# Attention state advanced on TensorE by diagonal products, and a list of work with its weight conversions moved

## The chip, the cores and the metric

One core of a Trainium2 chip. The metric is device time in microseconds (us) from launch to end, the median of several runs of the same kernel. A core has TensorE (PE in the rows; its weight loads are PEld), VectorE (DVE), ScalarE (ACT), GpSimd (POOL) and SyncE (SP), each with its own instruction queue, in order; a name with a q (SPq, ACTq) is the part of an engine that issues DMAs and waits. TensorE writes to PSUM, in banks of 128 partitions x 512 fp32.

## The reference

Three stages in a row, in fp32, checked against a numpy result.

```python
# attention: 2 batches, 8 heads, 768 positions, 64 per head; blocks of 64 in the reference
intra = (q_b k_b^T * Dmask) v_b              # Dmask[i,j] = lam^(i-j) for i >= j, else 0
inter = (q_b * lam^(pos+1)) kv_state
out_b = intra + inter
kv_state = lam^block * kv_state + (k_b * lam^(block-1-pos))^T v_b
# the 8 heads side by side: 1536 tokens x 512
h = x @ w_in;  y = (h * tanh(softplus(h))) @ w_out        # 512 -> 2048 -> 512 (Mish)
h = max(y @ w_in2, 0);  result = (h * h) @ w_out2         # 512 -> 2048 -> 512
```

## The kernel before

**Precision.** Every matrix of the two dense layers is held as a pair hi + lo: hi is the value rounded to TensorE's fast fp32r form, lo the rest. A product is three matmuls into one accumulator, `mm3` (L57): hi·hi (L58), hi·lo (L59), lo·hi (L60). Such a triple is called a group below.

**Weights.** Each layer has 16 slices of 128 hidden units; slices of both layers are numbered F = 0 to 31. A slice has two matrices (io = 0 into the hidden layer, io = 1 out of it), so there are 64 units, in the order of `units` (L67), eight to a set of four slices. They come from memory as 64-bit words, and a unit takes this chain, the conversion: load on SP into one of five raw buffers (`cv_load`, L73), a scaling on ACT (`cv_a`, L85), three VectorE operations (`cv_b`, L102, L104, L106), a cast on ACT that makes hi (`cv_h`, L117), a subtraction on POOL that makes lo (`cv_l`, L125). hi and lo live in a ring of eight slices: `cv_h` goes ahead only when the slice eight below has been used by all four token blocks. A call of `conv()` (L132) issues one cast and subtraction, one `cv_b`, one `cv_a` and one load, each for the unit that is next in its own counter.

**Dense layers.** 1536 tokens are four blocks of 384. A step is one block with one slice: stage 1 makes the hidden 128 x 384 (`m_h`, four groups), ACT applies Mish or Relu (`e_a`), hi and lo of it are made (`e_c`), stage 2 adds into the y banks (`m_y`; four groups in layer 1, three of width 512 in layer 2). Sixteen steps use one set of four slices; there are 128 steps.

**Attention.** Two heads make a pair; pair i is head pair i % 4 of token block i // 4, 16 pairs in all, three chunks of 128 positions in each. Blocks 0 and 2 begin a batch (`first`), 1 and 3 end it (`last`). A pair does: scores (`scores`, L223), scaling of k on ACT (L203) and of q on POOL (L210), a mask by the table of powers on VectorE (`mask`, L242, one for each score bank), updates (`update`, L214), the advance of the state (`advance`), the outputs (`outputs`, L255 and L259), then the result as hi (ACT, L268) and lo (VectorE, L272). From pair 4 on all pairs share the two banks X and Y: scores of the first head and the updates are in X, scores of the second head and the outputs in Y.

The state of a head is 64 x 64 and is advanced at each chunk, new = lam^128 x old + update. Before, that is one VectorE operation for each head (L237); for a first chunk it is a copy, head 0 on ACT, head 1 on VectorE (L235). Both updates of chunks 0 and 1 are issued together (`updates`), the third comes after the outputs.

**The list.** `plan()` names every operation of the attention, of the conversion of units 0 to 15, of steps 0 to 15 and of stage 1 of step 16, with engine, assumed duration, what it comes after, and for some a due time. `issue()` (L467) passes due times backwards, then repeatedly takes, over all engines, the operation that could start first by its own clock, among those within 0.25 us the one due first, and emits it. That fixes each engine's order; waits between engines follow from the data. At its end 19 units are loaded, 16 converted.

**The loop** (L522) takes steps 16 to 127. In step s it issues stage 1 and its activation for steps up to s + 3, `e_c(s+1)`, a call of `conv()` in odd steps, then stage 2 of step s. `weight()` (L139) gives a converted unit.

At the start the table of powers of lambda (`tables`, L179 and L182) is built on VectorE from lambda, loaded through ACT's DMA queue, and from an identity matrix that shares a buffer with later tiles.

Of the kernel before, what the change touches and what calls it, by code (L numbers as in the profile page):

```python
# [26 lines left out]
def tile_attn_mlp_mlp(ctx, tc, qkv_in, lam, w1i, w1o, w2i, w2o, out):  # L27
# [127 lines left out]
    head = [slice(0, D), slice(D, P)]  # L155
# [30 lines left out]
    class Pair:  # L186
# [38 lines left out]
        def updates(self):  # L225
            self.u = [self.S[0][:, N + c * D:N + (c + 1) * D] for c in range(2)]
            for c in range(2):
                self.update(self.u[c], c)

        def advance(self, c, u, js=(0, 1)):  # L230
            old, new = self.st[c], self.st[(c + 1) % NC]
            for j in js:
                d = head[j]
                if self.first and c == 0:
                    (dve.tensor_copy if j else act.copy)(new[d, d], u[d])  # L235
                else:
                    dve.scalar_tensor_tensor(  # L237
                        new[d, d], old[d, d], qs[d, self.p, P - 1:P], u[d], ALU.mult, ALU.add
                    )
# [30 lines left out]
        def leave_lo(self):  # L270
# [125 lines left out]
    def plan():  # L396
        NI = NB * NP
        step_due = lambda s: STEP0 + STEP * s
        op("lam", "ACTq", 0.1, [], lambda: act.dma_start(
            out=lam_b, in_=bass.AP(lam.tensor, lam.offset, [[0, P], [1, H]])))  # L400
        op("lp", "DVE", 0.4, ["lam"], lam_pairs)
        for p in range(NP):
            op(f"T{p}", "DVE", 1.2, ["lp"], lambda p=p: tables(p))
        for i in range(NI):
            a = pr[i]
            j = i - 1
            op(f"kq{i}", "SP", 1.05, [f"kq{j}", f"S{i-4}", f"QD{i-4}"], lambda i=i: load_kq(i))
            op(f"kv{i}", "SP", 1.05, [f"kv{j}", f"kq{i}", f"V{i-4}"], lambda i=i: load_kv(i))
            S_prev = [f"XL{j}", f"A2{j}"] if i > NP else [f"XL{i-3}", f"A2{i-3}"] if i == 3 else []
            if i == NP:  # L410
                S_prev = ["XL2", "A22"]
            op(f"S{i}", "PE", 0.75, [f"kq{i}"] + S_prev + [f"S{j}"], a.scores)
            op(f"KD{i}", "ACT", 0.85, [f"kv{i}", f"T{a.p}"], a.scale_k)
            op(f"QD{i}", "POOL", 1.05, [f"kq{i}", f"T{a.p}", f"V{i-3}"], a.scale_q)
# [3 lines left out]
            chain = [f"U{i}", f"V{i-2}", f"A2{i-2}"] + ([f"A2{i-4}"] if not a.first else [])  # L418
            if a.first:
                op(f"AC{i}", "ACT", 0.25, chain, lambda a=a: a.advance(0, a.u[0], (0,)))  # L420
                op(f"AD{i}", "DVE", 0.25, chain, lambda a=a: a.advance(0, a.u[0], (1,)))
                op(f"A{i}", "DVE", 0.56, [f"AC{i}", f"AD{i}"], lambda a=a: a.advance(1, a.u[1]))
            else:
                op(f"A{i}", "DVE", 1.12, chain, lambda a=a: [a.advance(c, a.u[c]) for c in range(2)])
            op(f"V{i}", "PE", 1.35, [f"P0{i}", f"A{i}", f"QD{i}", f"kv{i}"], a.outputs)
            own = step_due(i - 4.7) if i >= NP else None
            op(f"XH{i}", "ACT", 0.5, [f"V{i}"] + ([f"XH{j}"] if a.p else []), a.leave_hi)
            op(f"XL{i}", "DVE", 0.56, [f"XH{i}"], a.leave_lo, own)
            if not a.last:
                op(f"A2{i}", "DVE", 0.57, [f"V{i}", f"XL{i}"], a.leave_state, own)  # L430

        nu = 16
        for u in range(nu):
            F, io = units[u]
            op(f"W{u}", "SP", 1.4, [f"W{u-1}", f"CL{u-RAW}"], lambda u=u: cv_load(u))
            op(f"CA{u}", "ACT", 0.68, [f"W{u}", f"CA{u-1}", f"CC{u-2}"], cv_a)
            op(f"CB0{u}", "DVE", 0.45, [f"CA{u}", f"CC{u-1}"], lambda: cv_b(0))
            op(f"CB1{u}", "DVE", 0.72, [f"CB0{u}"], lambda: cv_b(1))
            op(f"CC{u}", "DVE", 0.72, [f"CB1{u}"], lambda: cv_b(2))
            op(f"CH{u}", "ACT", 0.66, [f"CC{u}", f"CH{u-1}"], cv_h)  # L440
            op(f"CL{u}", "POOL", 1.35, [f"CH{u}", f"CL{u-1}"], cv_l, None if F < 4 else step_due(3 + 1.6 * (u - 8)))
        for u in range(nu, nu + 3):
            op(f"W{u}", "SP", 1.4, [f"W{u-1}", f"CL{u-RAW}"], lambda u=u: cv_load(u), step_due(u - 4))
        unit = {units[u]: u for u in range(nu)}
        for s in range(AHEAD + 1):
            _, _, t, f, st, en = steps[s]
            w, wo = f"CL{unit[f, 0]}", f"CL{unit.get((f, 1))}"
            for a in range(KT):
                dep = [f"XL{NP*t+a}", w, f"MISH{s-2}" if a == 0 else f"HM{s}.{a-1}"]
                op(f"HM{s}.{a}", "PE", 0.53, dep, lambda s=s, a=a: m_h(s, [a]))  # L450
            op(f"MISH{s}", "ACT", 0.5, [f"HM{s}.{KT-1}"], lambda s=s: e_a(s))
            op(f"GH{s}", "ACT", 0.52, [f"MISH{s}", f"GH{s-1}", f"YM{s-2}.{KT-1}"], lambda s=s: e_hi(s))
            op(f"GL{s}", "POOL", 1.05, [f"GH{s}"], lambda s=s: e_lo(s), step_due(s) - 0.6)
            if s == AHEAD:
                break
            for e in range(KT):
                dep = [f"GL{s}", wo, f"YM{s}.{e-1}" if e else f"YM{s-1}.{KT-1}"]
                if st and t:
                    dep.append(f"YD{s-1}.{e}")
                if s == 0:  # L460
                    dep += ["XL0", "A20"] if e < 2 else ["XL1", "A21"]
                    dep += ["XL3", "A23"] if e < 2 else []
                op(f"YM{s}.{e}", "PE", 0.53, dep, lambda s=s, e=e: m_y(s, e), step_due(s) + 0.5 * e)
                if en:
                    op(f"YD{s}.{e}", "ACT", 0.5, [f"YM{s}.{e}"], lambda s=s, e=e: y_out(s, e), step_due(s + 1))

    def issue():  # L467
        names = list(ops)
        for n in reversed(names):
            o = ops[n]  # L470
            for a in o.after:
# [25 lines left out]
        if PLAN:  # L497
            for r, n, o in trace:
                print(f"{r:7.2f} {o.end:7.2f} {o.eng:4} {n:8} due {o.due:6.1f}")

    with tc.manual_schedule():
# [20 lines left out]
        for s in range(AHEAD, len(steps)):  # L522
# [65 lines left out]
```

## Time and profile before

| what | value |
|---|---|
| median of 3 runs | 649.22 us (647.98 to 650.6) |
| profiled execution | 650.57 us, its span 648.4 us |
| mean granted TensorE clock | 0.979 of full speed |
| TensorE busy | 607.6 us, 94% (3592 matmuls) |
| VectorE busy | 292.3 us, 45% |
| ScalarE busy | 231.4 us, 36% |
| GpSimd busy | 248.2 us, 38% |
| memory | 46.14 MB read, 3.15 MB written |

The span runs from the first to the last instruction. A busy share is over the whole span, and the stages differ: attention and its list at the front, the dense steps behind. Matmuls are pipelined, so their durations overlap; the spacing of starts tells their rate. An idle time belongs to the instruction behind it, with the engine that ended it.

### The profile page before, as it was taken

What the parts mean: (1) busy time and instruction counts of PE and PEld (TensorE: products, weight loads), DVE (VectorE), ACT (ScalarE), POOL (GpSimd) and SP (SyncE); (2) the same over time, 40 slices, a digit from 0 to 9 for tenths busy, and PEclk for the clock granted to TensorE, in tenths of its full rate; (3) what the DMA queues carried; (4) which work ended last, traced back from release to release, by engine and by line L of the source; (5) the groups of instructions that cost most, each with busy time, mean ns of one, the idle gap of its engine ahead of it and who ended that gap; (6) DMA issues with size and microseconds to landing.
All of it is one profiled execution on the core that took longest, in us unless ns stands there. A gap on an engine that the chain in (4) does not pass through costs nothing.

```text
span 648.4 us, 9101 instructions
## 1 busy us (share of the span) xinstructions
PE 607.6 (94%) x3592; PEld 560.3 (86%) x3592; DVE 292.3 (45%) x483; ACT 231.4 (36%) x486; POOL 248.2 (38%) x229
## 2 busy tenths in 40 slices
PE   7888989999999989998999989998999989998997
PEld 6777878999999979998999869987899879987996
DVE  5999974201444334442445534442555445440223
ACT  3465633332333323333344434433233323332111
POOL 2376542121344323343455434334233424434122
PEclk8799989999999989999999979999899999999999
DMA  8865641000011121111222111111211122000112
GB/s 308 294 233 197 215 150 69 1 1 1 16 58 61 62 66 54 58 59 60 66 66 66 38 60 65 55 55 55 67 58 53 51 66 66 33 1 0 50 50 97
DMA packets 15737, 49.86 MB, mean 77 GB/s; under 512 B 1872, under 2 KB 1872, under 8 KB 15696
## 3 DMA queue, kind: packets, MB, share of 16 engines
q1 hardware_dynamic: 15552, 49.29, 22.3%
q8 instruction: 28, 0.46, 0.3%
q14 instruction: 13, 0.11, 0.0%
q10 hardware_dynamic: 144, 0.00, 0.0%
HBM read 46.14 MB, written 3.15 MB: 76 GB/s over the span
## 4 chain that ended last, share of the span: by engine, by line
PE 48%; POOL 3%; issue 3%; DVE 0%; ACT 0%; POOLq 0%; ACTq 0%
PE y L59 9%; PE y L60 8%; PE y L58 8%; PE h L60 4%; PE h L58 4%; PE h L59 4%; PE Y L60 2%; PE Y L58 2%; PE Y L59 2%; POOL w L125 2%; PE X L60 1%; PE X L58 1%; PE X L59 1%; POOL gl L326 1%; DVE y L359 0%
## 5 line engine op out<-in xcount | busy, mean ns | idle before, releaser
L326 POOL TENSOR_TENSOR gl<-g,gh 128x384 fp32r<-128x384 f32 x64 | 67.0, 1046 | 180.8 <-ACT gh L319 175.9
L326 POOL TENSOR_TENSOR gl<-u,gh 128x384 fp32r<-128x384 f32 x64 | 67.7, 1059 | 168.8 <-ACT gh L316 98.4
L359 DVE TENSOR_TENSOR y<-y,y 128x384 f32<-128x384 f32 (+1 forms) x84 | 50.3, 612 | 122.2 <-PE y L60 122.0
L58 PE MATMUL h<-xh,w 128*128 128x384 f32 x288 | 98.3, 341 | 0.1
L60 PE MATMUL h<-xh,w 128*128 128x384 f32 x288 | 97.3, 338 | 0.5 <-POOL w L125 0.5
L59 PE MATMUL h<-xl,w 128*128 128x384 f32 x288 | 96.9, 336 | 0.0
L104 DVE SCALAR_TENSOR_TENSOR raw<-absw,raw 128x512 uint32<-128x512 uint32 x64 | 59.1, 924 | 80.9 <-ACT absw L93 76.6
L308 ACT ACTIVATE u<-h 128x384 f32<-128x384 f32 x72 | 35.4, 492 | 163.9 <-PE h L60 82.9
L125 POOL TENSOR_TENSOR w<-raw,w 128x512 fp32r<-128x512 f32 x64 | 85.7, 1339 | 16.4 <-ACT w L117 16.4
L58 PE MATMUL y<-gh,w 128*128 128x384 f32 x256 | 87.8, 343 | 3.2 <-ACT w L117 3.2
L60 PE MATMUL y<-gh,w 128*128 128x384 f32 x256 | 86.6, 338 | 2.4 <-POOL w L125 2.4
L59 PE MATMUL y<-gl,w 128*128 128x384 f32 x256 | 86.4, 338 | 1.7 <-POOL gl L326 1.7
L59 PE MATMUL y<-w,gh 128*128 128x512 f32 x192 | 77.7, 405 | 5.2 <-POOL w L125 5.2
L58 PE MATMUL y<-w,gh 128*128 128x512 f32 x192 | 76.1, 396 | 6.3 <-ACT w L117 6.3
L60 PE MATMUL y<-w,gl 128*128 128x512 f32 x192 | 77.1, 402 | 0.0
L58 PEld LDWEIGHTS h<-xh,w 128*128 128x128 f32 x288 | 54.4, 189 | 2.6 <-issue 0.3
L59 PEld LDWEIGHTS h<-xl,w 128*128 128x128 f32 x288 | 54.3, 189 | 1.3
L60 PEld LDWEIGHTS h<-xh,w 128*128 128x128 f32 x288 | 54.3, 188 | 1.3 <-POOL w L125 1.3
L106 DVE SCALAR_TENSOR_TENSOR raw<-raw 128x512 uint32<-128x512 uint32 x64 | 52.5, 820 | 2.1
L58 PEld LDWEIGHTS y<-gh,w 128*128 128x128 f32 x256 | 48.6, 190 | 5.2 <-ACT w L117 3.8
L60 PEld LDWEIGHTS y<-gh,w 128*128 128x128 f32 x256 | 48.6, 190 | 3.1 <-POOL w L125 3.1
L59 PEld LDWEIGHTS y<-gl,w 128*128 128x128 f32 x256 | 48.6, 190 | 2.3 <-POOL gl L326 2.3
(86 smaller groups left out, 1005.6 us busy)
## 6 DMA issues: line engine op xcount, KB each, us to landing
raw<-in_w1i_dram SPq DMA_DIRECT2D x16, 512.0 KB, 4.2
raw<-in_w1o_dram SPq DMA_DIRECT2D x16, 512.0 KB, 3.6
raw<-in_w2i_dram SPq DMA_DIRECT2D x16, 512.0 KB, 3.2
raw<-in_w2o_dram SPq DMA_DIRECT2D x16, 512.0 KB, 3.3
kq<-in_qkv_dram SPq DMA_DIRECT2D x16, 384.0 KB, 4.4
kv<-in_qkv_dram SPq DMA_DIRECT2D x16, 384.0 KB, 4.2
out_dram<-y SPq DMA_DIRECT2D x12, 256.0 KB, 2.0
lam_t<-in_lam_dram ACTq DMA_DIRECT2D x1, 4.0 KB, 5.2
```

Of the source, the lines that this page charges most:

```text
L58: pe.matmul(o, lhsT=wh, rhs=xh, start=start, stop=False)
L59: pe.matmul(o, lhsT=wh, rhs=xl, start=False, stop=False)
L60: pe.matmul(o, lhsT=wl, rhs=xh, start=False, stop=stop)
L104: dve.scalar_tensor_tensor(lo, a, 3, lo, ALU.logical_shift_left, ALU.bitwise_or)
L106: dve.scalar_tensor_tensor(lo, hi, 0x80000000, lo, ALU.bitwise_and, ALU.bitwise_or)
L125: pool.tensor_tensor(lo, raw.pop(u).bitcast(F32)[:, :, 0], hi.bitcast(F32), ALU.subtract)
L308: act.activation(u, h, AF.Relu if steps[s][1] else AF.Mish)
L326: pool.tensor_tensor(gl, g, gh.bitcast(F32), ALU.subtract)
L359: dve.tensor_tensor(o, o, y[:, :w], ALU.add)
```

## The change

- Lambda is loaded by SP, ahead of all other loads there, instead of by ACT's queue.
- The identity has a buffer of its own, and `dg` holds for each head pair the identity scaled by lam^128, row by row (one ACT operation per head pair, DG).
- The state is advanced in PSUM: behind each update product comes a second, diagonal matrix times old state, into the same accumulator; then two copies take it to SBUF, head 0 on ACT and head 1 on VectorE (`keep`). The second update comes after the copies of the first.
- In the list, the conversion of units 8 to 15 (slices 4 to 7) waits for the outputs of pair u, and its due times are later; loads reach unit 20, and units 16 and 17 go through the scaling and the three VectorE operations. Some assumed durations and due times differ.
- The loop calls `conv()` in steps 16 and 18 as well.

```diff
-    ident = gp.tile([P, N], F32, tag="g", name="ident")[:, :P]
+    ident = const.tile([P, P], F32, name="ident")
+    dg = ac.tile([P, NP, P], F32, name="dg")
...
         def update(self, o, c):
+            old = None if self.first and c == 0 else self.st[c]
             for j in range(2):
-                pe.matmul(o[head[j]], lhsT=self.kd[:, c, j], rhs=self.v_[:, c, j], start=True, stop=True)
+                pe.matmul(
+                    o[head[j]], lhsT=self.kd[:, c, j], rhs=self.v_[:, c, j], start=True, stop=old is None
+                )
+                if old is not None:
+                    pe.matmul(
+                        o[head[j]], lhsT=dg[:, self.p, head[j]], rhs=old[:, head[j]], start=False, stop=True
+                    )
+        def keep(self, c, o, j):
+            new = self.st[(c + 1) % NC]
+            (dve.tensor_copy if j else act.copy)(new[head[j], head[j]], o[head[j]])
...
-        op("lam", "ACTq", 0.1, [], lambda: act.dma_start(
+        op("lam", "SP", 0.45, [], lambda: sp.dma_start(
...
-            op(f"U{i}", "PE", 0.4, [f"S{i}", f"KD{i}"], a.updates)
...
-                op(f"A{i}", "DVE", 1.12, chain, lambda a=a: [a.advance(c, a.u[c]) for c in range(2)])
-            op(f"V{i}", "PE", 1.35, [f"P0{i}", f"A{i}", f"QD{i}", f"kv{i}"], a.outputs)
-            own = step_due(i - 4.7) if i >= NP else None
+            if a.first and a.p == i:
+                op(f"DG{i}", "ACT", 0.3, [f"T{i}"], lambda p=i: act.activation(
+                    dg[:, p], ident, AF.Copy, scale=qs[:, p, P - 1:P]))
+            us, c_prev = {}, [f"V{i-2}", f"AA2{i-2}", f"AD2{i-2}"]
+            c_prev += [] if a.first else [f"AA2{i-4}", f"AD2{i-4}", f"DG{a.p}"]
+            for c in range(2):
+                op(f"U{c}{i}", "PE", 0.3, [f"S{i}", f"KD{i}"] + c_prev,
+                   lambda a=a, c=c, us=us: us.update({c: a.step_state(c)}))
+                op(f"AA{c}{i}", "ACT", 0.23, [f"U{c}{i}"], lambda a=a, c=c, us=us: a.keep(c, us[c], 0))
+                op(f"AD{c}{i}", "DVE", 0.23, [f"U{c}{i}"], lambda a=a, c=c, us=us: a.keep(c, us[c], 1))
+                c_prev = [f"AA{c}{i}", f"AD{c}{i}", f"DG{a.p}"]
+            op(f"V{i}", "PE", 1.35, [f"P0{i}", f"QD{i}", f"kv{i}"] + c_prev, a.outputs)
+            own = step_due(i - 4.2) if i >= NP else None
...
-            op(f"CA{u}", "ACT", 0.68, [f"W{u}", f"CA{u-1}", f"CC{u-2}"], cv_a)
+            op(f"CA{u}", "ACT", 0.68, [f"W{u}", f"CA{u-1}", f"CC{u-2}"] + ([f"V{min(u, NI-1)}"] if F >= 4 else []), cv_a)
...
-            op(f"CL{u}", "POOL", 1.35, [f"CH{u}", f"CL{u-1}"], cv_l, None if F < 4 else step_due(3 + 1.6 * (u - 8)))
-        for u in range(nu, nu + 3):
-            op(f"W{u}", "SP", 1.4, [f"W{u-1}", f"CL{u-RAW}"], lambda u=u: cv_load(u), step_due(u - 4))
+            op(f"CL{u}", "POOL", 1.4, [f"CH{u}", f"CL{u-1}"], cv_l, None if F < 4 else step_due(9.5 + 0.8 * (u - 8)))
+        for u in range(nu, nu + 5):
+            op(f"W{u}", "SP", 1.4, [f"W{u-1}", f"CL{u-RAW}"], lambda u=u: cv_load(u), step_due(u - 3))
+        for u in range(nu, nu + 2):
+            op(f"CA{u}", "ACT", 0.68, [f"W{u}", f"CA{u-1}", f"CC{u-2}", f"V{NI-1}"], cv_a)
+            op(f"CB0{u}", "DVE", 0.55, [f"CA{u}", f"CC{u-1}"], lambda: cv_b(0))
+            op(f"CB1{u}", "DVE", 0.95, [f"CB0{u}"], lambda: cv_b(1))
+            op(f"CC{u}", "DVE", 0.95, [f"CB1{u}"], lambda: cv_b(2), step_due(u - 0.5))
...
-            if s % 2:
+            if s % 2 or s < AHEAD + 4:
                 conv()
```

## Rows read from the trace of the kernel before

**Rows 1.** Busy time by engine in three stretches: us (instructions), granted clock, DMA share, GB/s.

```profile
30.50:92.00 61.50, 53.81 (x459) 46.54 (x457) 58.70 (x95) 35.55 (x75) 38.76 (x29) 0.97 0.64 210
92.00:123.00 31.00, 31.00 (x300) 27.24 (x299) 11.15 (x31) 8.67 (x18) 6.89 (x7) 1.00 0.16 56
145.60:217.00 71.40, 71.31 (x412) 70.99 (x410) 25.20 (x36) 23.87 (x50) 23.36 (x23) 1.00 0.12 38
```

**Rows 2.** All waits of TensorE's matmuls from 145.6 to 643.2: total, times, longest.

```profile
PE y L58 <- ACT w L117: 9.5, 6, 1.6
PE Y L60 <- POOL w L125: 6.0, 6, 1.0
PE y L59 <- POOL w L125: 5.2, 4, 1.3
PE y L60 <- POOL w L125: 2.4, 2, 1.2
```

**Rows 3.** Timeline around one such place: start, duration, engine, what, [idle before <-releaser].

```profile
524.51 0.64 ACT L117 CAST w<-raw 128x512 fp32r<-128x512 f32 x1
...
525.20 0.51 PE L58 MATMUL y<-w,gh 128*128 128x512 f32 x1 [1.58 <-ACT w L117]
525.65 1.29 POOL L125 TENSOR_TENSOR w<-raw,w 128x512 fp32r<-128x512 f32 x1
...
526.99 0.51 PE L59 MATMUL y<-w,gh 128*128 128x512 f32 x1 [1.29 <-POOL w L125]
```

**Rows 4.** Busy time by engine around three of these places, as in rows 1.

```profile
230.00:240.00 10.00, 7.19 (x32) 6.55 (x32) 2.48 (x5) 2.01 (x4) 2.65 (x3) 0.83 0.20 63
375.00:390.00 15.00, 12.12 (x47) 10.32 (x46) 3.90 (x8) 5.08 (x10) 4.35 (x4) 0.77 0.11 36
450.00:460.00 10.00, 7.13 (x28) 5.68 (x27) 3.73 (x7) 2.32 (x5) 2.25 (x2) 0.83 0.17 52
```

**Rows 5.** Line L58 alone, one instruction a group: TensorE busy, weight loads, clock.

```profile
97.12:103.88 6.76, 2.55 (x7) 1.31 (x7) 1.00 0.45 172
30.50:122.85 92.35, 31.83 (x87) 16.54 (x87) 0.98 0.48 158
```

**Rows 6.** The two longest waits of TensorE from 18 to 123, as in rows 2.

```profile
PE Y L223 <- DVE st L237: 3.0, 3, 1.6
PE Y L223 <- DVE xl L272: 2.8, 3, 1.1
```

**Rows 7.** Groups of VectorE instructions by line: busy us, mean ns, idle before.

```profile
L104 DVE SCALAR_TENSOR_TENSOR raw<-absw,raw 128x512 uint32<-128x512 uint32 x64 | 59.1, 924 | 80.9 <-ACT absw L93 76.6
...
L237 DVE SCALAR_TENSOR_TENSOR mid<-mid,qs,X 64x64 f32<-64x64 f32 x26 | 7.2, 278 | 0.7
```

**Rows 8.** Timeline of TensorE: a pair's updates and the dense products behind them.

```profile
78.97 0.45 PE L214 MATMUL X<-kv 128*64 128x64 f32 x8
79.35 0.44 PE L58 MATMUL h<-xh,w 128*128 128x384 f32 x1
79.63 0.34 PE L59 MATMUL h<-xl,w 128*128 128x384 f32 x1
79.81 0.34 PE L60 MATMUL h<-xh,w 128*128 128x384 f32 x1
```

**Rows 9.** Timeline of ACT and VectorE: two copies out of one bank.

```profile
10.18 0.21 ACT L235 COPY mid<-y 64x64 f32<-64x64 f32 x1 [2.17 <-DVE pm L242]
...
10.42 0.23 DVE L235 COPY mid<-y 64x64 f32<-64x64 f32 x1 [0.33 <-ACT mid L235]
```

**Rows 10.** The start: timeline, and one DMA issue of the page (KB, us to landing).

```profile
0.87 0.37 ACTq L399 DMA_DIRECT2D lam_t<-in_lam_dram  x1
...
4.90 1.65 PE L223 MATMUL y<-kq 64*128 64x128 f32 x12
...
6.04 0.34 DVE L172 COPY lam_t<-lam_t 64x4 f32<-64x4 f32 x2 [4.92 <-DMA lam_t<-in_lam_dram]
...
out_dram<-y SPq DMA_DIRECT2D x12, 256.0 KB, 2.0
```

More of the change, by code (lines that the diff above doesn't have):

```diff
@@ L223, in scores, with step_state @@
                     pe.matmul(self.S[j][:, o], lhsT=k[head[j], o], rhs=q[head[j], o], start=True, stop=True)
[L225 to L239, printed above, removed]
+        def step_state(self, c):
+            u = self.S[0][:, N + c * D:N + (c + 1) * D]
+            self.update(u, c)
+            return u
         def mask(self, j):
@@ L406, in plan @@
             j = i - 1
-            op(f"kq{i}", "SP", 1.05, [f"kq{j}", f"S{i-4}", f"QD{i-4}"], lambda i=i: load_kq(i))
+            op(f"kq{i}", "SP", 1.05, ["lam", f"kq{j}", f"S{i-4}", f"QD{i-4}"], lambda i=i: load_kq(i))
             op(f"kv{i}", "SP", 1.05, [f"kv{j}", f"kq{i}", f"V{i-4}"], lambda i=i: load_kv(i))
-            S_prev = [f"XL{j}", f"A2{j}"] if i > NP else [f"XL{i-3}", f"A2{i-3}"] if i == 3 else []
+            S_prev = [f"{x}{j if i > NP else i - 3}" for x in ("XL", "AA2", "AD2")] if i > NP or i == 3 else []
@@ L410, in plan @@
             if i == NP:
-                S_prev = ["XL2", "A22"]
+                S_prev = ["XL2", "AA22", "AD22"]
             op(f"S{i}", "PE", 0.75, [f"kq{i}"] + S_prev + [f"S{j}"], a.scores)
             op(f"KD{i}", "ACT", 0.85, [f"kv{i}", f"T{a.p}"], a.scale_k)
-            op(f"QD{i}", "POOL", 1.05, [f"kq{i}", f"T{a.p}", f"V{i-3}"], a.scale_q)
-            op(f"U{i}", "PE", 0.4, [f"S{i}", f"KD{i}"], a.updates)
+            op(f"QD{i}", "POOL", 1.2, [f"kq{i}", f"T{a.p}", f"V{i-3}"], a.scale_q)
@@ L416, in plan @@
             op(f"P1{i}", "DVE", 0.56, [f"S{i}", f"T{a.p}", f"V{i-2}"], lambda a=a: a.mask(1))
             op(f"P0{i}", "DVE", 0.56, [f"P1{i}"], lambda a=a: a.mask(0))
[L418 to L423, printed above, removed]
-                op(f"A{i}", "DVE", 1.12, chain, lambda a=a: [a.advance(c, a.u[c]) for c in range(2)])
@@ L429, in plan @@
             if not a.last:
-                op(f"A2{i}", "DVE", 0.57, [f"V{i}", f"XL{i}"], a.leave_state, own)
+                o = lambda a=a: a.S[1][:, N:N + D]
+                op(f"AA2{i}", "ACT", 0.23, [f"V{i}"], lambda a=a, o=o: a.keep(2, o(), 0), own)
+                op(f"AD2{i}", "DVE", 0.23, [f"V{i}"], lambda a=a, o=o: a.keep(2, o(), 1), own)
         nu = 16
@@ L435, in plan @@
             op(f"W{u}", "SP", 1.4, [f"W{u-1}", f"CL{u-RAW}"], lambda u=u: cv_load(u))
-            op(f"CA{u}", "ACT", 0.68, [f"W{u}", f"CA{u-1}", f"CC{u-2}"], cv_a)
-            op(f"CB0{u}", "DVE", 0.45, [f"CA{u}", f"CC{u-1}"], lambda: cv_b(0))
-            op(f"CB1{u}", "DVE", 0.72, [f"CB0{u}"], lambda: cv_b(1))
-            op(f"CC{u}", "DVE", 0.72, [f"CB1{u}"], lambda: cv_b(2))
+            op(f"CA{u}", "ACT", 0.68, [f"W{u}", f"CA{u-1}", f"CC{u-2}"] + ([f"V{min(u, NI-1)}"] if F >= 4 else []), cv_a)
+            op(f"CB0{u}", "DVE", 0.55, [f"CA{u}", f"CC{u-1}"], lambda: cv_b(0))
+            op(f"CB1{u}", "DVE", 0.95, [f"CB0{u}"], lambda: cv_b(1))
+            op(f"CC{u}", "DVE", 0.95, [f"CB1{u}"], lambda: cv_b(2))
             op(f"CH{u}", "ACT", 0.66, [f"CC{u}", f"CH{u-1}"], cv_h)
-            op(f"CL{u}", "POOL", 1.35, [f"CH{u}", f"CL{u-1}"], cv_l, None if F < 4 else step_due(3 + 1.6 * (u - 8)))
-        for u in range(nu, nu + 3):
-            op(f"W{u}", "SP", 1.4, [f"W{u-1}", f"CL{u-RAW}"], lambda u=u: cv_load(u), step_due(u - 4))
+            op(f"CL{u}", "POOL", 1.4, [f"CH{u}", f"CL{u-1}"], cv_l, None if F < 4 else step_due(9.5 + 0.8 * (u - 8)))
[3 more added lines that the diff above has]
+            op(f"CA{u}", "ACT", 0.68, [f"W{u}", f"CA{u-1}", f"CC{u-2}", f"V{NI-1}"], cv_a)
+            op(f"CB0{u}", "DVE", 0.55, [f"CA{u}", f"CC{u-1}"], lambda: cv_b(0))
+            op(f"CB1{u}", "DVE", 0.95, [f"CB0{u}"], lambda: cv_b(1))
+            op(f"CC{u}", "DVE", 0.95, [f"CB1{u}"], lambda: cv_b(2), step_due(u - 0.5))
         unit = {units[u]: u for u in range(nu)}
@@ L460, in plan @@
                 if s == 0:
-                    dep += ["XL0", "A20"] if e < 2 else ["XL1", "A21"]
-                    dep += ["XL3", "A23"] if e < 2 else []
+                    dep += ["XL0", "AA20", "AD20"] if e < 2 else ["XL1", "AA21", "AD21"]
+                    dep += ["XL3", "AA23", "AD23"] if e < 2 else []
                 op(f"YM{s}.{e}", "PE", 0.53, dep, lambda s=s, e=e: m_y(s, e), step_due(s) + 0.5 * e)
@@ L482, in issue @@
                         ops[a].end + (0 if ops[a].eng == o.eng != "SP" else LAT)
-                        + (LAND if ops[a].eng in ("SP", "ACTq") and o.eng != "SP" else 0) for a in o.after
+                        + (LAND if ops[a].eng == "SP" and o.eng != "SP" else 0) for a in o.after
                     ])
```

4 lines of the change are left out of this document (1 added, 3 removed).

## The prediction, made before the changed kernel was run

> **What bounds the kernel now.** I read the page first: its busy times and the 40 slices show TensorE as the busiest engine everywhere, so the question is where TensorE stands. The windows by stage answer it [rows 1]. From 145.6 to 217 us TensorE is busy 71.31 of 71.40 us at the full granted clock: 412 matmuls, 0.173 us each, or 0.52 us for one group of three (hi·hi, hi·lo, lo·hi). From 92 to 123 us it is full too. From 30.5 to 92 us it is not: VectorE is the full one there (58.70 of 61.50 us), and TensorE is idle for 7.7 us. So there are two stages with something to gain: the list (to 145.6 us), where VectorE holds TensorE back, and the loop behind it, which is full until 217 us.
>
> What stops TensorE in the loop is in its waits from 145.6 us to its last stretch [rows 2]: nothing but weights. 9.5 us on the ACT cast L117, 6.0 + 5.2 + 2.4 us on the POOL subtraction L125: 23.1 us in 18 waits. They come in six groups, one per new set of four slices, each with two places: about 1.0 us before a stage-1 product (the six of Y L60) and about 2.8 us before a stage-2 product. The timeline of one of them [rows 3] says why: cast, then TensorE's first product 0.05 us after the cast's end, then the subtraction 0.1 us after it on POOL, then TensorE again. The weights of the last slice arrive just in time, that is, late. Follow `conv` from the list's end. Before, 19 units are loaded and 16 fully converted, and a call is made in odd steps only: step 17 starts unit 16, step 21 casts it, step 21+2k casts unit 16+k. Step 35 needs unit 23 (slice 11, second matrix), and the cast stands in step 35, behind the stage-1 activation of step 38 on ACT. Eight units per sixteen steps is exactly the rate of use, so the lateness never goes: the same two places of each of the six later groups stand.
>
> After the long waits the granted clock falls: 0.83, 0.77 and 0.83 of full speed in three windows [rows 4], mixtures of 2.4 and 1.2 GHz. Times the window that is 1.7 + 3.45 + 1.7 = 6.9 us; weighted with TensorE's busy share in them, 5.2. I take 6.0.
>
> **The loop's part.** The list now also loads units 19 and 20 and carries units 16 and 17 through all three VectorE operations; steps 16 and 18 call `conv` too. Then step 16 casts unit 16, 17, 18 and 19 one each, and 19+2(k-3) casts unit 16+k: unit 23 in step 27, unit 31 in step 43, always eight steps ahead of its use (about 33 us at 8 groups a step) where it was level with it. The slot test of `cv_h` (all four blocks have used the slice eight below) holds: unit 24 needs stage 1 of step 28, issued in step 25, and is cast in 29. So the 18 waits and the clock behind them go: 23.1 + 6.0 = 29.1 us. The added work is hidden: the extra conversions of 16 and 17 lie on VectorE after the last attention pair, and in steps 16 to 19 VectorE, ACT and POOL are each busy about a third [rows 1]. If that cover failed, a conversion is three VectorE operations of some 0.92 us [rows 7], 2.8 us, and eight steps of lead pay for it. Next late is nothing that the rows show: no other wait of TensorE is in [rows 2]. Bounds: 23 (the clock gives nothing back) to 32 (6.9 of clock, and 18 restarts at 0.1).
>
> **The list's part.** First its ceiling. A pair in the full stage takes 6.76 us and holds seven groups [rows 5], so attention costs 6.76 - 7 x 0.52 = 3.12 us of TensorE per pair. The stretch from 30.5 to 122.85 us holds 87 groups [rows 5] and 11 pairs: 87 x 0.52 + 11 x 3.12 = 79.6 us. It took 92.35, so 12.8 us could go, of which the two largest waits, both for VectorE, are 5.8 [rows 6].
>
> VectorE: 64 scalar_tensor_tensor on the state go, at 0.278 us [rows 7] 17.8 us; 40 advances (8 first pairs x 3, 8 last x 2) need 40 copies at 0.23 [rows 9], of which 8 were there: +7.4. So -10.4 us, 0.65 a pair. ACT gains 32 copies at 0.21 [rows 9] and four 128x128 scalings, bounded by 0.2 and 0.8 each: about 8 us on an engine that was 58% busy [rows 1]. Units 8 to 15 (2.8 us of VectorE each) move out of the full stretch to behind pairs 8 to 15, where it was 64% idle. Their subtractions on POOL move with them, into a stretch with 6.9 of 31 us busy [rows 1]; their raw buffers come free later, so SP's loads of units 13 to 18 do too, and a pair's load may queue behind one of them, but pairs load four ahead. With all this VectorE stops being the bound, except while units 0 to 7 are converted. I take 10 of the 12.8.
>
> TensorE: 32 state updates get two diagonal products each, two instructions apiece: 128 instructions of 64 columns. The trace has no such product beside an update; the nearest are the updates themselves, 8 in 0.38 us [rows 8]. At that rate 6.1 us; with no overlap of the two halves twice that, 12; fully overlapped half, 3. I take 6.1, the rate of the row. The second update is now a visit of its own between groups: the first product after such a visit starts 0.28 us before the next instead of 0.18 [rows 8], so 0.1 on the way out and as much in, 0.2 x 16 = 3.2. Together 9.3; the first four pairs lie where TensorE is idle anyway, so 12/16 of it, 7.0, is on the path. Bounds 3.5 to 14.
>
> The chain. A pair now goes TensorE, copies, TensorE, copies, TensorE; before, one run of VectorE lay between. The copies of the two heads read one PSUM bank from two engines. The trace: ACT's copy at 10.18 waited for VectorE's mask of that bank, VectorE's own copy started 0.03 us after ACT's end [rows 9]. So one keep costs 0.21 + 0.03 + 0.23 = 0.47 us, not 0.23, and a mask of that bank (some 0.55) may come between. Two groups of 0.52 between the updates hide it; without them each keep stands about 0.5. I take nothing here beyond the 2.8 us of the 12.8 left in place; bounds 0 to 16 (32 x 0.5). The Trainium skill, in "PSUM — Partial Sum Buffer", section "PSUM bank collisions raise a hardware error", says otherwise for the chip: two engines may be in different 32-partition quadrants of one bank at the same time, and these two copies are in different halves. By that rule a keep would cost 0.23; the trace does not agree, as the second copy waited for the first. What the rule would give is rival 3.
>
> The start. Lambda, 4 KB, was issued on ACT at 0.87 us and VectorE began on it at 6.04, after the first 384 KB of k and q were in TensorE's hands at 4.90 [rows 10]. First on SP it leaves before all of that, at about 0.74, and lands between 2.7 (the shortest landing on the page, 2.0 us, [rows 10]) and 5.9 (5.2 us, as before). It delays SP's loads by one issue, about 0.4 us, pair 0's scores with them. Tables, masks and keys wait for lambda, and VectorE is the full engine behind it, so 0.1 to 3.3 us can go, less 0.4: I take 2.0, nearer the short landing since nothing is queued in front. VectorE's relief in pairs 0 to 4, 5 x 0.66, is partly hidden by data still landing: 1.0.
>
> List: -10 - 3.0 + 7.0 = -6.0 us; bounds -15 to +8.
>
> **The sum.** The profiled execution took 650.57 us (span 648.4 and 2.2 around it), 1.35 above the median of the three runs. 650.57 - 29.1 - 6.0 = 615.5; on the median's scale 614.1 us. I forecast 614.
>
> **Rivals.**
> 1. The loop's waits go and the list gives nothing: the diagonal products and extra visits cost at the upper rate (14) and the relief is 9 us. For it: TensorE is full from 92 us, so every added product there shows. Against: 7.7 us idle before 92 us. List +5: 650.57 - 1.35 - 29.1 + 5 = 625.
> 2. The lead does not hold: `cv_h` or the ring of five raw buffers keeps the last slice late and half the waits stay (the change then doesn't do what it says). Against: the slot test as counted above. 614 + 15 = 629.
> 3. The two copies of a keep run side by side: 40 x 0.24 us of chain go, and the list gives up to 6 us more: 608. Against it: [rows 9]. (The page of the Trainium skill that would have it so is "PSUM — Partial Sum Buffer", named above.)
> 4. Slower: the state's chain becomes the bound of the list. Each pair has two keeps in series with TensorE, each behind a mask and a conversion operation on VectorE (0.47 + 0.55 + 0.92 us, [rows 7, 9]) and TensorE's order has no group left to place: 2 x 2.0 = 4.0 us a pair, 16 pairs, 64 us on top of the forecast: 678. It decides from 35/16 = 2.2 us of standing per pair. For it: single-bank pairs from pair 4 on. Against: the seven groups per pair, and ACT's half is free.
>
> **How the numbers follow.** Forecast 0.64, with its own range 606 to 622; rival 1 0.17; rival 2 0.07; rival 3 0.07; rival 4 0.03; a cancellation of list loss and a half-kept lead near the old time 0.02. The range that leaves out 2 in 10 at most reaches from rival 3 to rival 1: 604 to 626. A measurement of this kernel can tell about 0.5% (3.2 us) from no change. Faster 0.94 (forecast and rivals 1 to 3, less a little), same 0.02, slower 0.04.
>
> **What would show it.** Right: TensorE's waits from the loop's start name neither L117 nor L125 and sum to under 2 us; granted clock 1.00 in every window of the loop; the loop's 497.6 us become 468 to 470; its start lies near 139 to 140 us instead of 145.6; VectorE under 85% busy from 50 us on; state copies on ACT and VectorE one after the other; VectorE's first table before 4.5 us. Wrong: waits for L125 again at 72 us intervals (lead), TensorE waiting for copies of the state in most pairs (chain), or a loop start after 146 us (list).

## The result, and the profile after

The changed kernel takes 611.09 us (median of 4 runs, 610.59 to 611.26), the kernel before 649.91 us beside it (647.98 to 654.5): a ratio of 0.939, 95% interval 0.934 to 0.944. The profiled execution took 611.19 us, its span is 609.4. From its page, the busy times and the rows of 40 slices for TensorE, VectorE and the granted clock:

```profile
span 609.4 us, 9365 instructions
...
PE 599.8 (98%) x3720; PEld 555.9 (91%) x3720; DVE 284.9 (47%) x451; ACT 238.4 (39%) x522; POOL 245.4 (40%) x229
...
PE   8999999999999999999999999999999999999997
...
DVE  6994556451644443344444754434555445222213
...
PEclk9999999999999999999999999999999999999999
```

TensorE is full in every slice but the first and the last, and the page prints the full clock in all of them; for the first 14 us the spacing of products says otherwise (run 10). The windows that answer to [rows 1], the last one from the loop's start to near its end:

```profile
30.50:92.00 61.50, 60.10 (x565) 50.23 (x564) 37.98 (x67) 32.91 (x81) 28.61 (x24) 1.00 0.57 185
92.00:123.00 31.00, 31.00 (x288) 26.22 (x287) 15.71 (x29) 14.51 (x34) 10.13 (x9) 1.00 0.21 67
139.80:604.20 464.40, 464.40 (x2482) 439.56 (x2481) 198.38 (x291) 165.92 (x346) 187.69 (x168) 1.00 0.16 54
```

In the first stretch TensorE is idle for 1.4 us where it was 7.7, and VectorE, the full engine there before with 58.70 us, has 37.98. In the loop TensorE is busy 464.40 of 464.40 us. From 100 us to the end the view of waits is empty: the four rows of [rows 2] are gone, and no other has come. What is left stands at the front (waits of TensorE from 0 to 150 us; total, times, longest):

```profile
PE X L217 <- ACT mid L228: 1.3, 1, 1.3
PE y L217 <- ACT dg L418: 1.2, 1, 1.2
PE X L521 <- DVE zero L518: 1.2, 1, 1.2
PE y L217 <- DVE mid L228: 0.8, 1, 0.8
PE y L262 <- DVE pm L245: 0.5, 1, 0.5
PE y L237 <- DMA kq<-in_qkv_dram: 0.3, 1, 0.3
```

To split list from loop I use one mark that all kernels have: ScalarE's activation of step 18, the first one out of bank X. It starts at 150.03 us before and at

```profile
144.02 0.49 ACT L308 ACTIVATE u<-X 128x384 f32<-128x384 f32 x1 [1.59 <-PE X L60]
```

after. The last matmul starts at 644.13 before and 604.75 after. So the list gave 6.01 us and the loop 33.37 (494.10 became 460.73). The prediction had 6.0 and 29.1.

The start, answering to [rows 10]: lambda's issue, VectorE's first use of it, and pair 0's scores.

```profile
0.74 0.37 SPq L399 DMA_DIRECT2D lam_t<-in_lam_dram  x1
...
3.78 0.34 DVE L173 COPY lam_t<-lam_t 64x4 f32<-64x4 f32 x2 [2.65 <-DMA lam_t<-in_lam_dram]
...
5.25 1.66 PE L237 MATMUL y<-kq 64*128 64x128 f32 x12 [0.28 <-DMA kq<-in_qkv_dram]
```

Lambda is in use 2.26 us earlier, the scores start 0.35 later. The state's copies, answering to [rows 9], VectorE and then ACT:

```profile
8.69 0.23 DVE L228 COPY mid<-y 64x64 f32<-64x64 f32 x1 [0.70 <-PE y L217]
8.95 0.20 ACT L228 COPY mid<-y 64x64 f32<-64x64 f32 x1 [1.58 <-DVE mid L228]
```

ACT's copy waits for VectorE's, out of the other half of the bank; at 52.16 and 52.40 it is the other way round. And the visit for a state update in a full stretch, answering to [rows 8]:

```profile
60.42 0.34 PE L60 MATMUL h<-xh,w 128*128 128x384 f32 x1
60.69 0.34 PE L217 MATMUL X<-kv 128*64 128x64 f32 x4
60.85 0.29 PE L221 MATMUL X<-mid,dg 128*64 128x64 f32 x4
61.07 0.44 PE L58 MATMUL h<-xh,w 128*128 128x384 f32 x1
61.35 0.34 PE L59 MATMUL h<-xl,w 128*128 128x384 f32 x1
```

From the last dense product's start to the next one's are 0.65 us and one more of 0.28 behind it, where two plain spacings are 0.36: 0.57 us for four update instructions, four diagonal ones and the visit.

### The profile page after: what moved, and what is told of

It reads as the page before. It is cut to its first block, busy times and chain, and to the rows that moved or that the text cites. A ratio compares the mean times of both kernels' runs of the same rounds, so it can differ in the third digit from the quotient of the medians.

```text
span 609.4 us, 9365 instructions
## 1 busy us (share of the span) xinstructions
PE 599.8 (98%) x3720; PEld 555.9 (91%) x3720; DVE 284.9 (47%) x451; ACT 238.4 (39%) x522; POOL 245.4 (40%) x229
## 4 chain that ended last, share of the span: by engine, by line
PE 95%; DVE 3%; DMA 1%; issue 1%; ACT 0%; SPq 0%; ACTq 0%
PE y L58 15%; PE y L59 14%; PE y L60 14%; PE h L58 9%; PE h L60 8%; PE h L59 8%; PE Y L60 3%; PE X L60 3%; PE X L58 3%; PE Y L58 3%; PE X L59 3%; PE Y L59 3%; PE X L237 1%; PE Y L262 1%; PE Y L258 1%; PE X L217 1%
## 5 line engine op out<-in xcount | busy, mean ns | idle before, releaser
L58 PE MATMUL h<-xh,w 128*128 128x384 f32 x288 | 98.9, 344 | 0.0
L125 POOL TENSOR_TENSOR w<-raw,w 128x512 fp32r<-128x512 f32 x64 | 84.7, 1324 | 9.1 <-ACT w L117 9.1
L58 PE MATMUL y<-gh,w 128*128 128x384 f32 x256 | 87.9, 343 | 0.0
L59 PE MATMUL y<-w,gh 128*128 128x512 f32 x192 | 75.8, 395 | 0.0
L58 PE MATMUL y<-w,gh 128*128 128x512 f32 x192 | 74.6, 389 | 0.0
L58 PEld LDWEIGHTS h<-xh,w 128*128 128x128 f32 x288 | 54.0, 188 | 3.4 <-issue 1.0
L106 DVE SCALAR_TENSOR_TENSOR raw<-raw 128x512 uint32<-128x512 uint32 x64 | 49.7, 777 | 2.0
L58 PEld LDWEIGHTS y<-gh,w 128*128 128x128 f32 x256 | 48.0, 188 | 2.1 <-issue 0.3
```

The lines of the kernel that those rows point to most:

```text
L58: pe.matmul(o, lhsT=wh, rhs=xh, start=start, stop=False)
L59: pe.matmul(o, lhsT=wh, rhs=xl, start=False, stop=False)
L106: dve.scalar_tensor_tensor(lo, hi, 0x80000000, lo, ALU.bitwise_and, ALU.bitwise_or)
L125: pool.tensor_tensor(lo, raw.pop(u).bitcast(F32)[:, :, 0], hi.bitcast(F32), ALU.subtract)
```

## The experiments

Theory: the loop's part is the lead of the conversion and nothing else, and the list's part is VectorE's relief less what the products cost TensorE. Twelve kernels; unless said otherwise each is the changed kernel with one thing different. "Mark" is the start of step 18's activation in the profiled run (changed kernel: 144.02).

**1. No lead.** The list's tail (three loads, no conversion of units 16 and 17) and the calls of before.

```
-        for u in range(nu, nu + 5):
+        for u in range(nu, nu + 3):
...
-        for u in range(nu, nu + 2):
...
-            if s % 2 or s < AHEAD + 4:
+            if s % 2:
```

> The changed kernel without its lead: the list's tail and the odd-step calls of the conversion are those of before; lambda, the later slices and the diagonal products stay. Theory (the stops are conversions that come level with their use): TensorE's waits for L117 and L125 return in six groups, loop about 497 us as before, list still ending near 140 us; 611.1 + 33 = 644 us (638 to 650). Rival (slices 4 to 7 or the list's new order had part in it): under 630 us.

646.18 us (642.10 to 650.24, 10 runs); ratio to before 0.995, 0.991 to 0.999. Mark at 143.16, last matmul at 636.09: the loop takes 492.93 us from the mark, 32.2 more than after. The waits of the loop are the four rows of [rows 2] again, to the tenth of a microsecond: 23.1 us in 18 waits. The granted clock is under 1.00 in three windows of ten us:

```profile
365.00:375.00 10.00, 7.13 (x26) 5.61 (x25) 1.92 (x2) 3.50 (x7) 5.08 (x4) 0.78 0.22 80
375.00:385.00 10.00, 10.00 (x46) 9.14 (x45) 4.05 (x8) 3.92 (x8) 2.36 (x3) 0.88 0.01 3
445.00:455.00 10.00, 9.19 (x38) 8.08 (x39) 5.28 (x9) 0.91 (x2) 1.99 (x2) 0.83 0.15 52
```

The theory holds, the rival is out. What the view of waits does not show can be read from the starts of the products. For each of them from the mark to the last I take the time to the next start, less the idle time in it, less the plain interval of the changed kernel's loop (0.174 us after a product of 384 columns, 0.231 after one of 512). In run 1 4.7 us are left right around the 18 stops, 0.26 for each, and 4.4 us in intervals at the lower clock; 23.1 + 4.7 + 4.4 is the 32.2. Before against after it is 23.1 + 4.6 + 5.7 = 33.4, 0.25 for each stop. (An interval right behind a stop and at the lower clock is counted with the clock: 0.7 and 1.0 us.) The spread of the runs goes with the mean clock: 642.1 to 644.0 us at 0.989, 644.7 to 647.8 at 0.984, 648.6 to 650.2 at 0.978.

**2. The lead alone**, on the kernel before (the same lines the other way).

> The kernel before with the lead alone: units 19 and 20 loaded, 16 and 17 converted in the list, calls in steps 16 and 18 too. Theory: loop 464 to 466 us, loop start at 145.7 us or a little later as the list carries 2 more conversions; 649.9 - 33 = 617 us (615 to 620). If the list part and the loop part were not independent (rival), the loop would stay over 470 us and the time over 622 us.

617.47 us (614.28 to 618.69); ratio 0.951, 0.947 to 0.955. Mark at 150.25, last matmul at 610.99: 460.74 us, the loop of after: it has the same length with either list. By medians the list's part is 6.4 us with the lead (run 2 to the changed kernel) and 3.3 without it (649.46 us for the kernel before, beside run 1, to run 1, whose runs spread over 8 us).

**3. The smallest lead.** The list's tail of before, and `if s % 2 or s == AHEAD:`.

> The changed kernel with the smallest lead that can be had: the list's tail is that of before, and one call of the conversion is added, in step 16, so that unit 23 is cast in step 33 instead of 35 (changed kernel: 27). Theory (each stop is the cast and the subtraction of one unit, about 2.8 us, and a step is some 4 us): two steps of lead cover it, no waits for L117 or L125, 611 us (610 to 613). Rival (the eight steps are needed, since each call's three stages stand behind other work): waits at a part of the places, 620 to 640 us.

610.49 us (610.24 to 610.59); ratio 0.941. No wait after 139 us; from the mark to the last matmul 460.73 us. One call, two steps earlier, buys the whole 33 us; of the change's eight steps of lead six are reserve.

**4. The state as before**: scalar_tensor_tensor on VectorE, no diagonal products; lambda first, later slices and lead stay.

```
-                    pe.matmul(
-                        o[head[j]], lhsT=dg[:, self.p, head[j]], rhs=old[:, head[j]], start=False, stop=True
-                    )
...
+                    dve.scalar_tensor_tensor(
+                        new[d, d], old[d, d], qs[d, self.p, P - 1:P], u[d], ALU.mult, ALU.add
+                    )
```

> The changed kernel with the state advanced as before (scalar_tensor_tensor on VectorE, no diagonal products): lambda first, slices 4 to 7 later and the lead stay. By the prediction's terms TensorE has 7.0 us less on its path and VectorE 10.4 us more. Theory of the prediction (VectorE is what the list waits for, and the products relieve it): list ends 2 to 6 us later than 139.8, time 613 to 617 us. Rival (moving slices 4 to 7, 22 us of VectorE out of its full stretch, is relief enough, and the products only cost TensorE): 604 to 609 us.

608.49 us (605.11 to 610.02); ratio 0.937, 0.933 to 0.941. The profiled run is the 605.11 one: mark at 137.70, 6.32 us ahead of the changed kernel, the loop again 460.73. The prediction's theory falls: from 30 us on VectorE is no longer the bound without the products either. Its windows, where [rows 1] had 58.70 us of VectorE:

```profile
30.50:92.00 61.50, 60.79 (x553) 52.74 (x552) 43.62 (x90) 34.51 (x74) 31.91 (x28) 1.00 0.55 180
92.00:123.00 31.00, 31.00 (x255) 27.69 (x254) 21.78 (x39) 13.69 (x26) 11.46 (x10) 1.00 0.25 85
```

But the runs spread over 4.9 us, those of the changed kernel over 0.7, and the early part is worse: TensorE is busy 8.10 us from 10 to 20 us and 7.56 from 20 to 30 (changed kernel 9.56 and 9.19).

**5. Slices 4 to 7 early**, as before; the products stay.

```
- [f"W{u}", f"CA{u-1}", f"CC{u-2}"] + ([f"V{min(u, NI-1)}"] if F >= 4 else []), cv_a)
+ [f"W{u}", f"CA{u-1}", f"CC{u-2}"], cv_a)
- cv_l, None if F < 4 else step_due(9.5 + 0.8 * (u - 8)))
+ cv_l, None if F < 4 else step_due(3 + 1.6 * (u - 8)))
```

> The changed kernel with slices 4 to 7 converted as early as before (their first conversion does not wait for an attention pair, and their due times are those of before); all else of the change stays. Theory now (moving 22 us of VectorE out of its full stretch is what gave the list its time; the products are a loss there): VectorE full again from 40 to 80 us, TensorE waiting for VectorE there, list 4 to 7 us later, 615 to 618 us. Rival (the products relieve VectorE enough by themselves, as the prediction's sum has it): 610 to 612 us.

612.09 us (610.86 to 612.43); ratio 0.941; mark at 144.92. My theory of that moment falls, the rival holds (0.09 us above its 612). From 40 to 60 us VectorE is 92% busy, and TensorE still 98%:

```profile
40.00:60.00 20.00, 19.62 (x175) 16.25 (x175) 18.38 (x26) 11.66 (x26) 11.57 (x10) 1.00 0.71 231
```

Runs 2, 4 and 5 with the changed kernel make a table of the two ways to relieve VectorE, the lead in place everywhere. Run 2 also has lambda on ACT and the list's assumed durations and due times of before, which no run changed alone:

| | slices 4 to 7 early | later |
|---|---|---|
| state on VectorE | 617.47 (run 2) | 608.49 (run 4) |
| diagonal products | 612.09 (run 5) | 611.09 (the change) |

Either alone comes within 1.0 us of the change or beats it; what the assumed durations have in that is open. By these medians the products gain 5.4 us where the slices are early (lambda and the durations included) and lose 2.6 where they are late.

**6. Lambda on ACT's queue** as before, pair 0's load not behind it.

> The changed kernel with lambda on ACT's queue as before, and nothing of the pairs' loads waiting for it. The prediction's term: first on SP is worth 2.0 us, so 613 us. The trace of the changed kernel has VectorE's first table 2.26 us earlier than before and pair 0's scores 0.35 us later, so 1.9 us if all of it stays on the path. Rival (TensorE is fed from other work until 40 us, so an earlier start is lost again): 611 us, no difference.

611.25 us (610.44 to 612.08); ratio 0.941; mark at 144.23, 0.21 later than with lambda first. The rival holds, within what the start's clock leaves (run 10): TensorE is at half rate in 8.0 to 14.8 us here, and until 14 us in the changed kernel. Against runs 3 and 10, which have lambda first and less of half rate, the time is 0.8 and 1.2 us longer. The first pairs are 0.3 to 0.6 us late (pair 3's output leaves at 24.12 instead of 23.62), and that is nearly gone by the loop.

**7 and 8. Products in the first four, and in the first six pairs**; the others advance their state on VectorE.

```
+DGP = 4        # run 8: 6
-            old = None if self.first and c == 0 else self.st[c]
+            old = None if self.first and c == 0 or self.i >= DGP else self.st[c]
...
+            if i >= DGP:      # both updates in one visit, then scalar_tensor_tensor
```

> The changed kernel with diagonal products for the first four pairs only; the other twelve advance their state with scalar_tensor_tensor as before. Theory: the products cost TensorE what they take where it is full (12 of 16 pairs of the 6.3 us by which the run without any product ended its list earlier), and in the first 30 us they cost nothing and keep TensorE busy, so that its clock stays granted there: 611.1 - 4.7 = 606.4 us, runs within 1.5 us of each other. Rival (the products do not matter to the clock, the spread of 605 to 610 us of the run without them comes from the later pairs): 605 to 610 us, as wide as that.

> As the run before, with the products in the first six pairs, which takes in the stretch from 30 to 40 us where VectorE is 91 per cent busy and TensorE is not full. Theory: 611.1 - 6.3 x 10/16 = 607.2 us if the two pairs more only cost; 605.5 us if VectorE's relief in that stretch is worth the two pairs' products and more.

Four: 609.39 us (608.66 to 609.68); ratio 0.937. Six: 604.37 us (604.02 to 604.72); ratio 0.930, 0.928 to 0.932. Four is 3.0 us above its theory; six is below both of its figures. Six pairs is better than either whole way, and its runs agree within 0.7 us. Four fails where pairs 4 and 5 stand on a full VectorE. Its windows of ten us from 40, and then those of six:

```profile
40.00:50.00 10.00, 9.44 (x77) 7.95 (x75) 9.74 (x14) 5.10 (x11) 7.08 (x6) 1.00 0.65 221
50.00:60.00 10.00, 8.99 (x73) 8.13 (x75) 4.56 (x10) 3.68 (x8) 3.31 (x3) 0.83 0.54 181
```

```profile
40.00:50.00 10.00, 9.85 (x89) 8.43 (x87) 8.66 (x14) 5.06 (x11) 5.91 (x6) 1.00 0.83 273
50.00:60.00 10.00, 10.00 (x94) 8.58 (x95) 4.51 (x12) 4.72 (x12) 2.49 (x3) 1.00 0.59 174
```

With four, VectorE has 9.74 us of the first ten, TensorE then waits 3.3 us in three waits for VectorE's x_lo (one row of its waits from 30 to 60 us; line 287 is the L275 of the changed kernel), and behind that the clock is granted at 0.83:

```profile
PE Y L249 <- DVE xl L287: 3.3, 3, 1.8
```

**9. Every diagonal product twice** (`stop=False` on the first of the two).

> The changed kernel with every diagonal product issued twice (the old state is added twice, so the values are not the reference's): 128 more instructions of 64 columns on TensorE in the visits that are there already, nothing else. It prices the products alone. At the rate that the prediction took (0.048 us each, 6.1 us, of which 12/16 on the path) 4.6 us more, 615.7 us; at the other bounds 613.4 (fully overlapped halves) and 620 us (no overlap). The run with products in six pairs only gave 6.7 us for 20 updates, 0.34 each with their visit, so of 20 updates here 0.2 each is likeliest: 615 us.

617.27 us (616.97 to 617.92), 6.2 more than the changed kernel; mark at 149.96, 5.94 later. 5.94 / 128 = 0.046 us a product. But in the changed kernel's trace TensorE is at half rate until 14 us (run 10). Run 3 has the start of run 9 (pair 0's scores take 0.94 us in both, and the clock is granted at 0.50 from 8.4 to 11.8 us in both): against it the mark is 6.66 later, 0.052 a product, and pair 4 leaves 1.66 later (30.58 against 28.92), again 0.052 for each of the first 32. So the rate of [rows 8], 0.048, was nearly right, and the early products are not covered.

**10. Both key-value products of an update first, then both diagonal ones.**

```
-            for j in range(2): key-value product j, diagonal product j
+            for j in range(2): key-value product j
+            for j in range(2): diagonal product j
```

> The changed kernel with the four products of an update in another order: both heads' key-value products first, then both diagonal ones (they lie in different halves of the partitions). Theory (the price is TensorE's visit and the pipeline, not the order): 610.5 to 611.5 us. Rival (consecutive products of different halves overlap, those of one half do not): up to 0.1 us per update, 32 updates, 608 us.

610.04 us (609.99 to 610.34); ratio 0.940; mark at 142.88, 1.14 earlier. 0.83 of that is there when pair 4 leaves (28.95), and in run 3, which has the old order, pair 4 leaves at 28.92 too and the mark is 143.30. So the gain is one of the start, not a price per update. The spacing of TensorE's products shows what differs there. The scores of pair 1, 12 products, in the changed kernel's trace and in run 10's:

```profile
8.50 1.65 PE L237 MATMUL y<-kq 64*128 64x128 f32 x12
```

```profile
8.39 0.94 PE L237 MATMUL y<-kq 64*128 64x128 f32 x12
```

And four output products later in the changed kernel's trace:

```profile
11.20 0.65 PE L258 MATMUL y<-qd,mid 128*64 128x128 f32 x4
11.63 0.65 PE L262 MATMUL y<-pm,kv 128*64 128x128 f32 x4
```

Four products take 0.43 us there, as in the kernel before from 11.05 to 11.48 us, where the clock is granted at 0.50, and 0.22 in run 10 (13.52 to 13.74). So the changed kernel's trace is at the lower of the clock's two levels until about 14 us, though the view of windows prints 1.00 for that stretch. Run 10 is at full rate from pair 1's scores on, run 3 from 11.8 us. At the start the spacing has to be read, not the printed clock.

**11. Products in eight pairs**, DGP = 8.

> The changed kernel with diagonal products for the first eight pairs (the best so far has six). Theory (from pair 6 on TensorE is full and products only cost, 0.34 us an update): four updates more, 604.4 + 1.3 = 605.7 us. Rival (VectorE at 63 to 70 per cent in that stretch still holds up a pair now and then): 604 us or less.

604.93 us (604.62 to 607.47); ratio 0.933; mark at 137.15 against 136.77 with six. The direction is the theory's, but the size (0.4 to 0.6 us) is less than half of the 1.3 and within the spread of the runs.

**12. Six pairs, and the order of run 10.**

> The two best together: products in the first six pairs only, and within an update both key-value products ahead of both diagonal ones. Theory: 604.4 us, and of the 1.0 us that the order of the halves gave over 32 updates the share of the 10 or so updates with products left, 0.3 us: 604.1 us (603.5 to 604.7), 0.93 of the kernel before. Rival (the 1.0 us came from the early pairs, where the chain is waited for): 603.4 us.

604.76 us (604.72 to 605.77, 5 runs); ratio 0.933, 0.930 to 0.935. No gain over run 8, which agrees with run 10's gain being none of the updates'. Run 8 is the fastest version: 0.930 of the kernel before, 6.7 us under the changed kernel, with no overlap of the runs, and 6.1 under run 3, which has its rate at the start.

## Why the prediction came out as it did

The time was 611.1 us for 614, inside the forecast's own range; the direction and both parts' signs were right.

**The loop, -29.1 forecast, -33.4 measured.** Mechanism right at every step: the waits for L117 and L125 are gone, the clock is 1.00 throughout, run 1 brings back the same 18 waits and run 2 removes them alone. The term was mis-sized. The waits were taken at what the view shows as idle, 23.1 us, and restarts (18 at 0.1) only went into the bound. By the account of run 1 4.6 us more belong to the stops. The place of [rows 3], with the two products ahead of it (TensorE, kernel before), is an instance:

```profile
523.11 0.33 PE L59 MATMUL X<-xl,w 128*128 128x384 f32 x1
523.28 0.34 PE L60 MATMUL X<-xh,w 128*128 128x384 f32 x1
```

The product at 525.20 has 1.58 us of idle before it, counted from the end of the one at 523.28, 523.62. But the plain spacing is 0.17, so it could have started at 523.45. The stop is 1.75 us, 0.17 more than shown. And the product that had to wait is itself followed later than plain, by 0.28 for 0.17 us:

```profile
217.93 0.45 PE L60 MATMUL Y<-xh,w 128*128 128x384 f32 x1 [1.02 <-POOL w L125]
218.21 0.34 PE L58 MATMUL Y<-xh,w 128*128 128x384 f32 x1
218.39 0.33 PE L59 MATMUL Y<-xl,w 128*128 128x384 f32 x1
```

The clock, taken at 6.0, is 5.7. So what the sum lacked is the 4.6 us around the stops.

**The list, -6.0 forecast, -6.0 measured, and that is luck.** Up to the mark TensorE has the same instructions in every kernel, 1134, but for the products. So the mark is TensorE's idle time plus its busy time, and part of the busy time is at half rate. The windows up to the mark, each followed by those at half rate (at the start by the spacing of products, as in run 10, though the view prints 1.00). Before, then run 4, then the change:

```profile
0.00:150.03 150.03, 136.19 (x1134) 120.60 (x1135) 93.78 (x184) 65.50 (x141) 62.73 (x62) 0.95 0.46 159
0.00:6.59 6.59, 5.37 (x20) 3.88 (x20) 0.77 (x4) 1.49 (x2) 1.83 (x13) 1.00 0.54 160
10.01:13.42 3.41, 3.28 (x34) 3.10 (x36) 2.56 (x9) 1.41 (x5) 1.23 (x2) 0.50 1.03 404
23.66:30.49 6.83, 6.29 (x46) 5.33 (x47) 6.51 (x16) 1.58 (x4) 2.62 (x2) 0.50 0.63 204
88.52:91.93 3.41, 3.41 (x22) 3.07 (x23) 3.22 (x6) 0.77 (x2) 0.84 (x2) 0.50 0.37 96
```

```profile
0.00:137.70 137.70, 130.03 (x1134) 113.38 (x1135) 90.25 (x190) 67.25 (x144) 59.60 (x62) 1.00 0.51 173
0.00:6.74 6.74, 5.32 (x20) 3.85 (x20) 3.25 (x9) 1.84 (x3) 2.83 (x14) 1.00 0.63 186
```

```profile
0.00:144.02 144.02, 138.71 (x1262) 120.17 (x1263) 84.91 (x158) 73.96 (x180) 58.75 (x62) 1.00 0.49 165
0.00:14.08 14.08, 11.42 (x86) 9.44 (x86) 8.52 (x23) 5.62 (x15) 4.88 (x17) 1.00 0.84 304
```

| TensorE up to the mark, us | before | run 4 | the change |
|---|---|---|---|
| idle | 13.84 | 7.67 | 5.31 |
| busy | 136.19 | 130.03 | 138.71 |
| of that at half rate | 18.35 | 5.32 | 11.42 |
| work: busy less half of that | 127.0 | 127.4 | 133.0 |

Products at half rate take at most twice the time, so at most half of that time is lost. In single profiled runs the terms are:

| term | forecast | measured, before to the change |
|---|---|---|
| relief of VectorE, other waits, the start | -10 - 3.0 | -8.5 of idle time |
| TensorE's clock up to the mark | no term | -3.5 at most |
| diagonal products and visits | +7.0 | +6.0 |

The relief fell 4.5 us short of its forecast; the clock, which the list's sum had left out, and somewhat cheaper products made up for it. Of the kernel before's time at half rate, 9.6 us lie from 10 to 30.5, ahead of the stretch that the ceiling of 12.8 us was worked out for. Run 4's list ends 12.3 us ahead of the kernel before, and half of that too is clock (6.5 at most, idle time 6.2). From run 4 to the change it is 6.3, but run 4's trace is the fastest of its four runs, and 3.0 of the 6.3 are half rate at the start; by medians it is 2.6.

Two steps of the prediction failed inside this sum. One gave lambda 2.0 us: it did start VectorE 2.26 us earlier, but little of that stayed on the path. In run 6 TensorE's first wait behind pair 0's scores is 2.3 us, for the scaled keys, where in the changed kernel it is 1.2, for the diagonal matrix; pair 4 leaves 0.54 us later (30.32), and the mark is 0.21 later. The other put the relief down to both edits together, while the table of runs 2, 4 and 5 shows that they stand in for each other. In the stretch of the ceiling, 30.50 to 122.85, TensorE is idle for 7.7 us before, 0.7 in run 4 and 1.4 with the change. So behind the first 30 us later slices alone take away the idle time, and the products on top only cost; ahead of that they help, as run 8 with its six pairs shows. That could have been seen: units 8 to 15 are 8 x 2.8 = 22 us of VectorE by [rows 7], twice the 10.4 us of the copies, and the full stretch needed 58.70 us in 61.50. And the products of the first four pairs are not free on TensorE, as the prediction took them: one more costs 0.052 us there as elsewhere (run 9).

**The chain** cost little, as taken: TensorE's waits for copies of the state sum to 2.1 us in two waits, both on the first pairs. The copies do go one after the other, though in different halves of a bank. The Trainium skill ("PSUM — Partial Sum Buffer", "PSUM bank collisions raise a hardware error") allows different 32-partition quadrants of one bank at the same time; in this program the second copy waited for the first, 0.47 us a keep. The rows name the first copy as what released the second, and the profile infers releasers from semaphore events. So the program's own waits stood there, and the trace does not speak against the page, as the prediction had it; whether the chip would run them side by side was not tried.

**Rivals.** 1 (list +5) is wrong by 11 us, 2 (half the waits stay) is out as none does, 3 by the copies' order, though 611.1 lies as near to its 608 as to 614, by the loop's larger gain, 4 by the 2.1 us.

**The signs.** Loop start 139.8 (forecast 139 to 140), VectorE at most 74% busy in windows of ten us from 50 us on (120 to 130; under 85), first use of lambda at 3.78 (under 4.5): as forecast. The loop's length was not: 464.4 for 468 to 470.

## What to carry to other kernels

A pipeline that is served at exactly the rate of its use never recovers from starting late; look for the same stop at the same place of every round, and give it one turn of lead: here one call was worth 33 us. Two edits that relieve the same engine are not to be added: once one of them has moved the bound, the other is priced on the new one, and a mixture by place (products where VectorE is full, VectorE where TensorE is) beat both. When a stop is priced, take the spacing of starts on both sides of it less the plain spacing, not the idle time shown. And where two traces are compared, look first at whether TensorE ran at the same rate in both.

## What the runs showed of the hardware

- A stop of TensorE costs 0.25 to 0.26 us more than the idle time that the profile puts before the next matmul (18 stops: 4.6 us before, 4.7 in run 1): 0.17 ahead of the product that waits and some 0.1 behind it.
- The loop at the full clock is exact: 460.73 or 460.74 us from the mark to the last matmul in the changed kernel and runs 2 to 12. What differs between these traces lies ahead of the mark.
- Without products TensorE is 76 to 81% busy from 10 to 30 us, and runs lie between 605.1 and 610.0 us; with products in the first six pairs it is 91 to 97% busy and they lie within 0.7 us. The mean granted clock of the four wide runs is 1.00, 0.999, 0.994 and 0.988, but the one at 0.999 took 607.8 us. The mean does not count the start (the changed kernel's trace has 0.999 with half rate until 14 us), so how much of the spread is clock is open.
- How long TensorE's start is at half rate differs between traces, and the view of the clock does not show it: pair 0's 12 scores take 1.65 or 1.66 us in the changed kernel and in runs 4, 5 and 10, and 0.94 in runs 3, 6, 8 and 9. In the changed kernel and run 5 half rate goes on until about 14 us; in runs 3, 8 and 9 the view shows 0.50 later, from about 8.4 to 11.8 us.
